# VectorE exp tiles planned eight units ahead in a fused attention and gated-MLP block

## The chip, the cores and the metric

The kernel runs on one core of a Trainium2 chip. The metric is the time of one execution on the device in microseconds (us). Before the change it is 927.56 us, the median of 4 runs (927.19 to 927.69).

## The reference

One transformer block on a sequence of 2048 tokens of width 640, one batch, bf16 inputs. Layer norm, attention with 32 heads of size 20, residual, layer norm, gated MLP of width 1728, residual:

```python
x = A_x                                               # [1, 2048, 640]
qkv = layernorm(x) @ wqkv                             # 32 heads, Dh = 20
p = softmax(q k^T * Dh ** -0.5)                       # per head 2048 x 2048
h = x + (p v, heads joined) @ wo
n = layernorm(h)
out = h + (gelu_tanh(n @ w_gate) * (n @ w_up)) @ w_down
```

## The kernel before

**Tiling.** The queries are cut into seven chunks of 512, 512, 256, 256, 256, 128 and 128 rows (`CHUNKS`). Heads go in groups of four, since four heads of 20 rows fit in the 128 rows of TensorE's array. A *slot* is one chunk with one head group (512 rows), two groups (256) or four (128); so every slot has 64 score tiles of 128 x 512, and there are 32 slots (8, 8, 4, 4, 4, 2, 2 by chunk). In the code and in the diff "group" in "end of a group" is such a slot.

**Units.** The tiles that ScalarE exponentiates are taken in *units* of alternately three and two tiles, 719 units in all, numbered here from 0. `unit(u)` (line 833) queues one: the score matmuls (L852, into PSUM banks 0 to 2 or 3 and 4), one ScalarE exp over the whole unit (L339, PSUM to the buffers `pts` or `rege`), and then the PV matmuls (L339 too, `ps<-pts,v_all` or `ps<-rege,v_all`), which add up P times V in PSUM bank 6. The exp buffers hold 18 tiles, about seven units: an exp must wait for the PV that reads the tiles it overwrites. The scores of unit u reuse the banks of unit u-2, so they wait until exp u-2 is done.

**VectorE exp tiles.** Eight of a slot's 64 tiles (two in the first slot) are exponentiated by VectorE instead: 250 tiles. Their scores go to a free bank (7 or 5), VectorE reads them (L812, one 128 x 512 instruction a tile), and for each pair of tiles it runs seven instructions of 1024 columns (bit arithmetic on int16, L339) in `d_exp`. The pair buffers hold four pairs. `dtile[u]` names the VectorE tile that goes with unit u; `D_FIRST` and `D_SPAN` spread a slot's tiles over its units. A finished tile joins the PV of a unit that is at least `D_LAG` = 8 units later; at the last PV of a slot all that are left are flushed.

**Slot end.** `epilogue` copies bank 6 out (`osb`), transposes it (L962), and multiplies by the reciprocal of the row sums (L968, L971) into `o_nat`. After a chunk's last slot, `post` does that chunk's output projection (L616, `wo`), residual, LN2, gate matmuls (L1039), gelu (ScalarE, with table loads for gelu and back to exp), up matmuls (L1039, multiplied by VectorE at L1085), down matmuls (L1096) and output. That work is spread among the exps of the following chunks; that of the last chunk (`tail`) runs after the last exp, with gelu straight from PSUM (L1061, L1064).

**What sets the order.** Every operation is put into `Sched` with its engine, an estimated duration, a priority and its dependences. `schedule()` walks time with those estimates, lets each engine take the ready operation of best priority (scores 0, PV 1, epilogue and VectorE tiles 2, output projection and LN2 2.5, background 3), and so fixes one instruction order per engine; `emit` writes it with semaphore waits. Nothing is reordered on the chip: an instruction that waits holds what is queued behind it on its engine.

**Zero matmuls.** Two rules in `schedule()` add matmuls that change nothing. When a PV operation is placed and PE's planned use over the last 3.4 us is under `PAD_MIN`, groups of four matmuls with a zero stationary operand into bank 6 are put behind it (`ps<-kt_all,zer`, L339). When PE has nothing ready and the use is under `WARM_MIN`, one such group, or one 128 x 512 matmul into bank 7 (`ps<-kt_all`), is put in.

The two lines that the change turns most on:

```python
want = min(nd, (k[0] - D_FIRST) * nd // D_SPAN + 1) if k[0] >= D_FIRST else 0   # VectorE tiles due by unit k[0] of a slot
if len(quads) < PV_QUADS and not final:      # PV_QUADS = 2: a PV waits until it has two quads of tiles
```

Of the kernel before, what the change touches and what calls it, by code (L numbers as in the profile page):

```python
# [14 lines left out]
SEM_LAT = {("act", "pe"): 0.056, ("dve", "pe"): 0.058, ("pe", "act"): 0.045, ("pe", "dve"): 0.038}  # L15
SEM_ANY = 0.036
DRAIN = {"pe": 0.165, "act": 0.115, "dve": 0.085, "pool": 0.05, "sp": 0.0}
WARM_WIN, WARM_MIN = 3.4, 0.5
PAD_WIN, PAD_MIN = 3.4, 0.42
PE_AGE = 1.5  # L20

MODE_SWITCH = {"pe": 0.105, "act": 1.28}
# [19 lines left out]
class Sched:  # L42
# [12 lines left out]
    def op(self, eng, fns, dur, prio, reads=(), writes=(), acq=(), rel=(), after=(), sem=None, lat=None, mode=None, util=0.0):  # L55
        o = Op()
        o.i = len(self.ops)
        o.eng, o.dur, o.lat, o.sem = eng, dur, DRAIN[eng] if lat is None else lat, sem
        o.util = util
        o.mode = mode  # L60
        o.tag = writes[0] if writes else None
        o.fns = fns if isinstance(fns, list) else [fns]
        o.prio = (prio, o.i)
        deps = set(after)
        for r in reads:
            if r in self.lw:
                deps.add(self.lw[r])
        for w in writes:
            if w in self.lw:
                deps.add(self.lw[w])  # L70
            deps.update(self.rd.get(w, ()))
        for r in reads:
            self.rd.setdefault(r, []).append(o.i)
        for w in writes:
            self.lw[w] = o.i
            self.rd[w] = []
        deps.discard(o.i)
        o.deps = deps
        o.acq = list(acq)
        o.rel = list(rel)  # L80
        o.succ = []
        o.ready = 0.0
        self.ops.append(o)
        return o.i

    def schedule(self):
# [22 lines left out]
        while done < total:  # L109
# [4 lines left out]
            for e in ENGINES:  # L114
                while future[e] and future[e][0][0] <= t + 1e-9:
                    _, p, i = heapq.heappop(future[e])
# [6 lines left out]
                while ready[e]:  # L123
                    p, i = heapq.heappop(ready[e])
                    o = ops[i]
# [35 lines left out]
                if chosen is None:  # L161
                    if e == "pe" and self.warm is not None:
# [5 lines left out]
                        if sum(x for _, x in recent) < WARM_MIN * WARM_WIN and (free7 or live):  # L168
                            o = Op()
# [14 lines left out]
                o = chosen  # L184
                if e == "pe" and self.pad is not None and o.tag and o.tag[0] == "O":
                    while recent and recent[0][0] < t - PAD_WIN:
                        recent.popleft()
                    u = sum(x for _, x in recent) + o.util
                    while u < PAD_MIN * PAD_WIN and o.util < 1.1:
                        o.fns = o.fns + self.pad  # L190
                        o.dur += 0.215
                        o.util += 0.213
                        u += 0.213
                    live = o.i not in self.final
# [100 lines left out]
CHUNKS = tuple((sum(SIZES[:i]), n) for i, n in enumerate(SIZES))  # L295
# [10 lines left out]
PV_QUADS = 2  # L306
D_LAG = 8
# [1 line left out]
ND = 4  # L309
D_PER_SLOT = (8,) * len(SIZES)  # L310
D_SLOT0 = 2
D_FIRST, D_SPAN = 1, 16
RSQRT_MAGIC = float(0x5F3759DF)

P_QK, P_PV, P_PRO, P_EPI, P_LN, P_BG = 0, 1, 1.5, 2, 2.5, 3
# [2 lines left out]
def bass_sequential_preLN__mha_block__glu_gated_geglu__prompt_kernel(  # L318
# [12 lines left out]
    with ExitStack() as es:  # L331
# [6 lines left out]
        def I(method, *args, **kwargs):  # L338
            return lambda eng: getattr(eng, method)(*args, **kwargs)  # L339
# [414 lines left out]
        slots = []  # L754
        for c, (q0, nq) in enumerate(CHUNKS):
            n = 512 // nq
            slots += [(c, tuple(range(g, g + n))) for g in range(0, NG, n)]

        tiles = []
# [4 lines left out]
            slot_end.append(len(tiles))  # L764

        PAT = [((0, 1, 2), (3, 4))] * len(CHUNKS)
        units, ubank, dtile, ends = [], [], [], []
        i, in_slot = 0, {}
        while i < len(tiles):
            s_ = tiles[i][0]  # L770
            c = slots[s_][0]
            bs = PAT[c][len(units) % 2]
            k = in_slot.setdefault(s_, [0, 0])
            nd = D_PER_SLOT[c] if s_ else D_SLOT0
            units.append(tiles[i:i + len(bs)])
            ubank.append(bs[0])
            i += len(units[-1])
            want = min(nd, (k[0] - D_FIRST) * nd // D_SPAN + 1) if k[0] >= D_FIRST else 0
            if k[1] < want and tiles[i][0] == s_:
                dtile.append(tiles[i])  # L780
                k[1] += 1
                i += 1
            else:
                dtile.append(None)
            k[0] += 1
            ends.append(i)
        assert all(k[1] % 2 == 0 for k in in_slot.values())
        d_tiles = set(x for x in dtile if x)
        x_unit = {}
        for u, tl in enumerate(units):  # L790
# [2 lines left out]
        pv_bank = {}  # L793
# [3 lines left out]
        d_raw, d_done = [], []  # L797
# [33 lines left out]
        def unit(u):  # L831
            tl = units[u]
# [8 lines left out]
            pb, o = (pts, p0) if p0 < PR else (pts2, p0 - PR)  # L841
# [35 lines left out]
            n = 512 * na  # L877
# [6 lines left out]
            while pv_wait:  # L884

                quads = []
                while pv_wait and len(quads) < PV_QUADS:
                    x0 = pv_wait[0][2]
                    have = [x for x in pv_wait if x[2][:3] == x0[:3]]
                    want = 4 - sum(1 for j in range(4) if x0[:3] + (j,) in d_tiles)  # L890
                    if len(have) < want or quads and quads[0][0][2][0] != x0[0]:
                        break
                    del pv_wait[0:want]
                    quads.append(have)
                if not quads:
                    return
                s_ = quads[0][0][2][0]
                c, gs = slots[s_]
                q0, nq = CHUNKS[c]
                nk = 512 // nq  # L900
                final = quads[-1][0][2][1:3] == (gs[-1], NT // nk - 1)
                if len(quads) < PV_QUADS and not final:
                    pv_wait[0:0] = [x for h in quads for x in h]
                    return

                for have in quads:
                    for x in list(d_done):
                        if u - x_unit[x[2]] >= D_LAG and x[2][3] not in [y[2][3] for y in have]:
                            have.append(x)
                            d_done.remove(x)  # L910
                while final and d_done:
                    have = []
                    for x in list(d_done):
                        if x[2][3] not in [y[2][3] for y in have]:
                            have.append(x)
                            d_done.remove(x)
                    quads.append(have)
                if s_ not in pv_bank:
                    pv_bank[s_] = bk = Bank(6)
                    acq = [bk]  # L920
                else:
                    bk, acq = pv_bank[s_], []
                fns, reads = [], ["vones", "zer"] + k_keys[0][0]
                for have in quads:
                    for kk in range(nk):
                        for pt, pkey, (_, g, kb, j) in have:
                            kt = kb * nk + kk
                            o = 512 * 6 + nq * gs.index(g)
                            fns.append(I("matmul", PS[32 * j:32 * j + VW, o:o + nq], v_all[:, kt, 4 * g + j, :],
                                         pt[:, kk * nq:(kk + 1) * nq], start=(s_, j) not in pv_open, stop=(kt == NT - 1),  # L930
                                         tile_position=(0, 32 * j), skip_group_check=True))
                            pv_open.add((s_, j))
                            reads += [pkey, ("v", kt, g // 4)]
                pv = op("pe", fns, 0.218 * len(quads), P_PV, mode="col", util=0.213 * len(quads), reads=reads, writes=[("O", s_), "pvseq"], acq=acq)
                if final:
                    sc.final.add(pv)
                    assert not d_done and not d_raw
                    epilogue(s_, bk)


        def base(c):
            n = CHUNKS[c][1]
            if n == 128:
                return 2 + (c == len(CHUNKS) - 1)
            return 2 * (c % 2) if n < 512 else 0

        def epilogue(s_, bk):
            s = s_ % 2
# [29 lines left out]
        def prefetch(c):  # L978
            q0, nq = CHUNKS[c]
            nt = nq // 128  # L980
            tb = base(c)
            op("sp", I("dma_start", h_sb[:, tb:tb + nt, :], x_hbm[q0:q0 + nq, :].rearrange("(t p) d -> p t d", p=128)), 0.08, P_EPI,
               writes=[("h", tb + tt, hf) for tt in range(nt) for hf in range(2)], sem=f"xr{c}", lat=2.0 + nq * 0.0034,
               after=tuple(e_ops) + tuple(w_readers) if c == 0 else ())

        def post(c, banks, tail):
            p = P_EPI if tail else P_LN
            q0, nq = CHUNKS[c]
            nt = nq // 128
            tb = base(c)  # L990
            hb = 1792 * tb
            first = tuple(e_ops) + tuple(last_qk[0]) + tuple(d_ops) if c == 0 else ()
# [129 lines left out]
        for s_, (c, gs) in enumerate(slots):  # L1122
# [27 lines left out]
            while ui < len(units) and ends[ui] - len(units[ui]) < slot_end[s_]:  # L1150
                unit(ui)
                ui += 1
# [35 lines left out]
```

## Time and profile before

| | |
|---|---|
| median of 4 runs | 927.56 us (927.19 to 927.69) |
| profiled execution | 927.6 us, of which the span from first to last instruction is 925.6 us |
| ScalarE (ACT) | 885.7 us busy, 96% |
| TensorE (PE) | 845.5 us busy, 91%; granted clock 1.000 |
| VectorE (DVE) | 810.4 us busy, 88% |
| DMA | 34.36 MB, 37 GB/s on the mean |
| first exp starts, last exp ends | 35.93 us, 889.49 us |
| exps of 1536 and of 1024 columns | 1590 and 1170 ns each, overlapping: 2.26 us for one of each on the chain |

The page gives busy times over the whole span. The views by stage split it at the first and the last exp. "L339" is the line of the helper that records most operations, so its groups are told apart by engine and by the names behind it (output`<-`inputs). PEld is TensorE's weight load, which runs beside the matmuls. A line's "idle before" is the time in which its engine had nothing running, and the name behind `<-` is what ended it.

### The profile page before, as it was taken

The numbers are of one execution on the slowest core, as the hardware profiler recorded it, in microseconds if no ns is written. First come the engines' busy times: TensorE is split into PE (matmuls) and PEld (weight loads), VectorE is DVE, ScalarE is ACT, GpSimd is POOL, SyncE is SP. The second block draws the span as 40 slices with busy tenths as digits, with TensorE's granted clock in tenths as the row PEclk, the third lists the DMA queues.
The fourth block names the chain that finished last, engine by engine and source line by source line (L and its number), as shares of the span: only waits on it lengthen the run. The fifth ranks groups of instructions, "written<-read, shape, count | busy, mean of one in ns | idle before, by whom it ended". The sixth has DMA issues, their size and how long they took to land.

```text
span 925.6 us, 23154 instructions
## 1 busy us (share of the span) xinstructions
PE 845.5 (91%) x10109; PEld 354.9 (38%) x10109; DVE 810.4 (88%) x1703; ACT 885.7 (96%) x801; POOL 35.1 (4%) x117
## 2 busy tenths in 40 slices
PE   3998999999998998999888999999989999999998
PEld 2432222222232222233233333344444445555667
DVE  7859999999898998888798997989998997998873
ACT  6899999999999999999999999999999999999962
POOL 5000000000001000000001000001000000000100
DMA  7211010322550000001011000000100000110000
GB/s 256 87 26 44 18 55 18 90 60 66 147 185 16 15 1 1 1 15 44 1 31 23 9 2 1 16 30 10 37 16 16 8 23 2 31 32 10 10 17 16
DMA packets 39517, 34.36 MB, mean 37 GB/s; under 512 B 19436, under 2 KB 36936, under 8 KB 39416
## 3 DMA queue, kind: packets, MB, share of 16 engines
q1 hardware_dynamic: 39416, 32.89, 12.6%
q8 instruction: 79, 1.29, 0.6%
q14 instruction: 22, 0.18, 0.1%
HBM read 20.12 MB, written 8.09 MB: 30 GB/s over the span
## 4 chain that ended last, share of the span: by engine, by line
ACT 72%; PE 14%; DVE 11%; issue 1%; POOL 0%; DMA 0%
ACT pts L339 46%; ACT rege L339 25%; PE ps L1039 4%; DVE qt_all L339 3%; PE ps L616 3%; PE ps L852 3%; PE ps L339 3%; DVE rege L339 2%; PE ps L1096 2%; DVE qt_all L812 1%; DVE rege L812 1%; DVE stats L339 1%; ACT L339 1%; DVE rege L1074 1%; PE ps L561 0%
## 5 line engine op out<-in xcount | busy, mean ns | idle before, releaser
L339 ACT ACTIVATE pts<-ps 128x1536 bf16<-128x1536 f32 x480 | 573.1, 1380 | 4.9 <-PE ps L852 3.7
L852 PE MATMUL ps<-qt_all,kt_all 32*128 32x256 bf16 (+2 forms) x3584 | 303.4, 289 | 43.1 <-ACT pts L339 27.4
L339 ACT ACTIVATE rege<-ps 128x1536 bf16<-128x1536 f32 x239 | 300.1, 1381 | 1.9 <-PE ps L339 1.5
L852 PEld LDWEIGHTS ps<-qt_all,kt_all 32*128 32x128 bf16 x3584 | 95.1, 92 | 276.8 <-ACT pts L339 161.1
L339 DVE TENSOR_TENSOR qt_all<-qt_all 128x1024 bf16<-128x1024 bf16 (+1 forms) x240 | 164.1, 684 | 3.4
L1039 PE MATMUL ps<-rege,regw 128*128 128x256 bf16 (+2 forms) x980 | 154.6, 290 | 9.9 <-ACT rege L339 4.1
L339 PE MATMUL ps<-pts,v_all 128*21 128x256 bf16 (+2 forms) x2098 | 138.8, 290 | 0.5 <-DVE rege L339 0.5
L812 DVE TENSOR_SCALAR rege<-ps 128x512 int16<-128x512 f32 x154 | 105.4, 685 | 27.6 <-PE ps L852 26.9
L339 DVE TENSOR_SCALAR qt_all<-qt_all 128x1024 bf16<-128x1024 int16 (+1 forms) x288 | 115.8, 417 | 2.5
L339 PE MATMUL ps<-rege,v_all 128*21 128x256 bf16 (+2 forms) x1294 | 113.3, 292 | 0.1
L1039 PEld LDWEIGHTS ps<-rege,regw 128*128 128x128 bf16 x980 | 72.5, 98 | 67.9 <-issue 28.5
L616 PE MATMUL ps<-regw 128*128 128x512 bf16 (+1 forms) x360 | 87.1, 352 | 2.0 <-DVE v_all L749 0.7
L1096 PE MATMUL ps<-regw,rege 128*128 128x320 bf16 x448 | 79.4, 301 | 1.1 <-DVE rege L1064 0.5
L812 DVE TENSOR_SCALAR qt_all<-ps 128x512 int16<-128x512 f32 x96 | 65.7, 685 | 3.7 <-PE ps L852 2.6
L339 DVE TENSOR_SCALAR rege<-rege 128x1024 int16<-128x1024 int16 (+2 forms) x166 | 67.2, 421 | 1.3
L339 DVE TENSOR_TENSOR rege<-rege 128x1024 bf16<-128x1024 bf16 (+3 forms) x103 | 65.5, 644 | 0.9
L339 PEld LDWEIGHTS ps<-pts,v_all 128*21 128x21 bf16 x2098 | 50.2, 91 | 37.2 <-issue 31.6
L339 PE MATMUL ps<-kt_all,zer 128*32 128x512 bf16 x676 | 56.6, 384 | 0.0
L1096 PEld LDWEIGHTS ps<-regw,rege 128*128 128x128 bf16 x448 | 36.7, 97 | 32.4 <-issue 15.8
L339 PEld LDWEIGHTS ps<-rege,v_all 128*21 128x21 bf16 x1294 | 41.0, 91 | 20.6 <-issue 14.3
L1085 DVE TENSOR_TENSOR rege<-rege,ps 128x512 bf16<-128x512 bf16 (+1 forms) x53 | 35.8, 676 | 12.1 <-PE ps L1039 11.8
L616 PEld LDWEIGHTS ps<-regw 128*128 128x128 bf16 x360 | 28.6, 99 | 45.4 <-issue 21.3
(95 smaller groups left out, 574.5 us busy)
## 6 DMA issues: line engine op xcount, KB each, us to landing
rege<-in_A_x_dram SPq DMA_DIRECT2D x6, 640.0 KB, 5.1
q_rows<-regw SPq DMA_DIRECT2D x20, 128.0 KB, 1.7
out_dram<-rege SPq DMA_DIRECT2D x16, 160.0 KB, 2.0
regw<-in_B_w_gate_dram SPq DMA_DIRECT2D x1, 2160.0 KB, 12.0
regw<-in_B_w_up_dram SPq DMA_DIRECT2D x1, 2160.0 KB, 17.0
regw<-in_B_w_down_dram SPq DMA_DIRECT2D x1, 2080.0 KB, 22.2
kt_all<-k_rows SPq DMA_DIRECT2D x12, 160.0 KB
qt_all<-q_rows SPq DMA_DIRECT2D x12, 160.0 KB
```

The source lines that it names most:

```text
L339: return lambda eng: getattr(eng, method)(*args, **kwargs)
L616: yield op("pe", lambda eng, l=l, r=r, k=k: eng.matmul(bank(bk, n), l, r, start=(k == 0), stop=(k == len(steps) - 1)), c_mm(n), prio, mode ...
L812: d_ops.append(op("dve", lambda eng: eng.tensor_scalar(v[:, 512 * h:512 * h + 512], bank(b), EXP_MUL, -32000.0, ALU.mult, ALU.max), c_dve( ...
L852: return lambda eng: eng.matmul(out()[:, kk * nq:(kk + 1) * nq], kt_all[32 * j:32 * j + 32, g, kt * 128:(kt + 1) * 128], qt_all[32 * j:32 ...
L1039: op("pe", lambda eng, a=a, f=f, fi=fi: eng.matmul(bank(bk)[:, fi * nq:(fi + 1) * nq], w[:, a, F0[f]:F0[f] + 128], hnT[:, a, 128 * tb:128 ...
L1074: cp.append(op("dve", lambda eng, bg=bg, fv=fv, w=w: eng.tensor_copy(fv, bank(bg, w)), c_dve(w), p, reads=[kg], writes=hkeys(k), rel=[bg], ...
L1085: hdone.append(op("dve", lambda eng, bu=bu, fv=fv, w=w: eng.tensor_tensor(fv, fv, bank(bu, w), ALU.mult), c_dve(w), p, reads=[ku] + hkeys( ...
L1096: op("pe", lambda eng, f=f, o=o, hf=hf, bk=bk: eng.matmul(bank(bk, 320), ha_f[:, o:o + 128], wd[:, f, hf * 320:(hf + 1) * 320], start=(f = ...
```

## The change

Four things change; none of the arithmetic does.

- The VectorE tiles of a slot are planned over 20 units instead of 16 (`D_SPAN`), and then each is taken eight units sooner (`D_LEAD`), so that a slot's first ones go with units of the slot before it. Chunk 1's don't go ahead of chunk 1's first unit. A finished tile that has waited 12 units or more (`D_LAG` + `D_HOLD`) gets a PV quad of its own, and tiles are only given to the PV of their own slot.
- A slot's first PV may have one quad instead of two.
- The thresholds of the zero matmuls rise: 0.42 to 0.5 behind a PV, to 0.6 behind a slot's last PV, and 0.5 to 0.55 where PE has nothing ready.
- `base()`, which places a chunk in the buffers of the MLP, is written in another way.

```diff
--- before.py
+++ after.py
@@ -15,8 +15,8 @@
 SEM_LAT = {("act", "pe"): 0.056, ("dve", "pe"): 0.058, ("pe", "act"): 0.045, ("pe", "dve"): 0.038}
 SEM_ANY = 0.036
 DRAIN = {"pe": 0.165, "act": 0.115, "dve": 0.085, "pool": 0.05, "sp": 0.0}
-WARM_WIN, WARM_MIN = 3.4, 0.5
-PAD_WIN, PAD_MIN = 3.4, 0.42
+WARM_WIN, WARM_MIN = 3.4, 0.55
+PAD_WIN, PAD_MIN, PAD_END = 3.4, 0.5, 0.6
 PE_AGE = 1.5
 
 MODE_SWITCH = {"pe": 0.105, "act": 1.28}
@@ -186,7 +186,8 @@
                     while recent and recent[0][0] < t - PAD_WIN:
                         recent.popleft()
                     u = sum(x for _, x in recent) + o.util
-                    while u < PAD_MIN * PAD_WIN and o.util < 1.1:
+                    want = PAD_END if o.i in self.final else PAD_MIN
+                    while u < want * PAD_WIN and o.util < 1.1:
                         o.fns = o.fns + self.pad
                         o.dur += 0.215
                         o.util += 0.213
@@ -309,7 +310,7 @@
 ND = 4
 D_PER_SLOT = (8,) * len(SIZES)
 D_SLOT0 = 2
-D_FIRST, D_SPAN = 1, 16
+D_FIRST, D_SPAN, D_LEAD, D_HOLD = 1, 20, 8, 4
 RSQRT_MAGIC = float(0x5F3759DF)
 
 P_QK, P_PV, P_PRO, P_EPI, P_LN, P_BG = 0, 1, 1.5, 2, 2.5, 3
@@ -764,7 +765,7 @@
             slot_end.append(len(tiles))
 
         PAT = [((0, 1, 2), (3, 4))] * len(CHUNKS)
-        units, ubank, dtile, ends = [], [], [], []
+        units, ubank, dplan, ends = [], [], [], []
         i, in_slot = 0, {}
         while i < len(tiles):
             s_ = tiles[i][0]
@@ -776,15 +777,20 @@
             ubank.append(bs[0])
             i += len(units[-1])
             want = min(nd, (k[0] - D_FIRST) * nd // D_SPAN + 1) if k[0] >= D_FIRST else 0
-            if k[1] < want and tiles[i][0] == s_:
-                dtile.append(tiles[i])
+            if k[1] < want and i < len(tiles) and tiles[i][0] == s_:
+                dplan.append((len(units) - 1, tiles[i]))
                 k[1] += 1
                 i += 1
-            else:
-                dtile.append(None)
             k[0] += 1
             ends.append(i)
         assert all(k[1] % 2 == 0 for k in in_slot.values())
+        chunk_u = [min(u for u, tl in enumerate(units) if slots[tl[0][0]][0] == c) for c in range(len(CHUNKS))]
+        dtile = [None] * len(units)
+        u = 0
+        for n, x in dplan:
+            u = max(n - D_LEAD, u, D_FIRST, chunk_u[1] if slots[x[0]][0] == 1 else 0)
+            dtile[u] = x
+            u += 1
         d_tiles = set(x for x in dtile if x)
         x_unit = {}
         for u, tl in enumerate(units):
@@ -899,19 +905,26 @@
                 q0, nq = CHUNKS[c]
                 nk = 512 // nq
                 final = quads[-1][0][2][1:3] == (gs[-1], NT // nk - 1)
-                if len(quads) < PV_QUADS and not final:
+                if len(quads) < PV_QUADS and not final and s_ in pv_bank:
                     pv_wait[0:0] = [x for h in quads for x in h]
                     return
 
                 for have in quads:
                     for x in list(d_done):
-                        if u - x_unit[x[2]] >= D_LAG and x[2][3] not in [y[2][3] for y in have]:
+                        if u - x_unit[x[2]] >= D_LAG and x[2][0] == s_ and x[2][3] not in [y[2][3] for y in have]:
                             have.append(x)
                             d_done.remove(x)
-                while final and d_done:
+                if any(x[2][0] == s_ and u - x_unit[x[2]] >= D_LAG + D_HOLD for x in d_done):
                     have = []
                     for x in list(d_done):
-                        if x[2][3] not in [y[2][3] for y in have]:
+                        if x[2][0] == s_ and u - x_unit[x[2]] >= D_LAG and x[2][3] not in [y[2][3] for y in have]:
+                            have.append(x)
+                            d_done.remove(x)
+                    quads.append(have)
+                while final and any(x[2][0] == s_ for x in d_done):
+                    have = []
+                    for x in list(d_done):
+                        if x[2][0] == s_ and x[2][3] not in [y[2][3] for y in have]:
                             have.append(x)
                             d_done.remove(x)
                     quads.append(have)
@@ -934,15 +947,16 @@
                 pv = op("pe", fns, 0.218 * len(quads), P_PV, mode="col", util=0.213 * len(quads), reads=reads, writes=[("O", s_), "pvseq"], acq=acq)
                 if final:
                     sc.final.add(pv)
-                    assert not d_done and not d_raw
+                    assert not any(x[0] == s_ for x in d_raw)
                     epilogue(s_, bk)
 
 
         def base(c):
             n = CHUNKS[c][1]
-            if n == 128:
-                return 2 + (c == len(CHUNKS) - 1)
-            return 2 * (c % 2) if n < 512 else 0
+            if n == 512:
+                return 0
+            half = sum(1 for _, m in CHUNKS[:c] if m == 256) % 2
+            return 2 * half + (n == 128 and CHUNKS[c - 1][1] == 128)
 
         def epilogue(s_, bk):
             s = s_ % 2
```

## The prediction

> **What bounds the kernel now.** I read the page first (share of each engine, chain that ended last), then busy time by stage, then ScalarE's own waits, then the timeline around the longest of them and around the end.
>
> ```profile
> PE 845.5 (91%) x10109; PEld 354.9 (38%) x10109; DVE 810.4 (88%) x1703; ACT 885.7 (96%) x801; POOL 35.1 (4%) x117
> ACT 72%; PE 14%; DVE 11%; issue 1%; POOL 0%; DMA 0%
> ```
>
> ScalarE carries the chain: 72% of the span.
>
> ```profile
> 35.90:250.00 214.10, 200.40 (x1593) 60.01 (x1592) 191.40 (x400) 211.61 (x187) 0.62 (x1) 1.00 0.20 54
> 250.00:889.50 639.50, 593.02 (x7940) 256.97 (x7938) 574.49 (x1174) 638.52 (x557) 22.39 (x84) 1.00 0.09 24
> 889.50:925.60 36.10, 30.73 (x428) 25.56 (x426) 14.33 (x35) 11.02 (x14) 0.00 (x0) 1.00 0.04 15
> ```
>
> The columns are stretch, length, then busy us (count) of PE, PEld, DVE, ACT, POOL, then the granted TensorE clock. Between 35.9 and 889.5 us, the exp stage, ScalarE is busy 850.1 of 853.6 us. In the last 36.1 us it is busy 11.0, and PE 30.7.
>
> ```profile
> ACT rege L339 <- PE ps L339: 1.5, 1, 1.5
> ACT pts L339 <- PE ps L339: 0.9, 2, 0.6
> ACT rege L339 <- PE ps L852: 0.4, 1, 0.4
> ```
>
> These are ScalarE's waits inside that stage (the one 3.7 us wait for L852 there is the first exp). A wait for "PE ps L339" is a wait for the PV matmuls that read an exp buffer which the next exp overwrites. The longest:
>
> ```profile
> 143.03 0.39 PE L852 MATMUL ps<-qt_all,kt_all 32*128 32x512 bf16 x2
> 143.36 0.60 PE L339 MATMUL ps<-pts,v_all 128*21 128x512 bf16 x5
> 144.44 2.37 ACT L339 ACTIVATE rege<-ps 128x1536 bf16<-128x1536 f32 x2 [1.46 <-PE ps L339]
> ```
>
> Exp 94 waits for 11 PV matmuls that stand in PE's queue behind the scores of unit 95, and those scores could only start when exp 93 was done: score wait, scores, 0.99 us of PV, 1.46 us idle. Last, the end, as the chain and then as ScalarE's timeline:
>
> ```profile
> 887.73 3.37 PE ps L1096 x24
> 891.32 1.00 PE ps L339 x48
> 902.51 2.79 PE ps L1039 x50
> 907.48 3.80 PE ps L1096 x28
> 911.28 7.05 PE ps L1039 x126
> 918.83 3.99 PE ps L1096 x28
> ```
>
> ```profile
> 895.72 0.70 ACT L567 ACTIVATE rege<-ps 128x640 bf16<-128x640 bf16 x1 [4.71 <-PE ps L561]
> 896.44 1.28 ACT L339 ACT_TABLE_LOAD   x1
> 900.59 1.70 ACT L339 ACTIVATE rege<-rege 128x1792 bf16<-128x1792 bf16 x1 [2.87 <-DVE rege L1074]
> 902.30 1.28 ACT L339 ACT_TABLE_LOAD   x1
> 903.59 0.20 ACT L339 ACTIVATE sd<-sd 128x1 bf16<-128x1 bf16 x1
> 905.62 0.70 ACT L567 ACTIVATE rege<-ps 128x640 bf16<-128x640 bf16 x1 [0.30 <-PE ps L561]
> ```
>
> The last exp ends at 889.49. Chunk 5's MLP then still owes 70 gate matmuls, its gelu and everything after; the last chunk's own MLP (the 126) starts only at 911.28.
>
> **The sum to work against.** 35.9 head + 853.6 exp stage + 36.1 tail = 925.6 span, 2.0 around it, 927.6 for the profiled run; the median is 927.56, so the two can be used alike.
>
> **The change, part by part.** I compared the instruction order of both programs as built. DVE has 1705 instructions in both, POOL 121, SP 180; 719 exps and 250 VectorE exp tiles in both. So ScalarE's exp work changes by 0. What differs: 272 more zero matmuls (68 groups of four), 18 more warm matmuls, one table load less (15 for 16), and the order.
>
> *Zero and warm matmuls.* 676 now are busy 56.6 us, 0.335 a group; 55 warm ones 16.7 us, 0.304 each. Added: 68 x 0.335 + 18 x 0.304 = 28.3 us of PE. The cover is PE's idle time before scores that wait for ScalarE, 161.1 + 77.2 us (PEld waits, L852): 238 us. Cost 0 while covered, up to 28.3 without. Few stretches get long: one gap between scores holds eight groups, others at most five. The gain is 0 too: the granted clock is 1.00 in every stretch, and no matmul group after 20 us runs at half rate. The Trainium skill ("TensorE: Matmul & The Clock Gate", "Part 1: The HAM clock gate") has PE fall to half clock after an idle window of some 3.4 us; by it the additions would insure matmuls, but this trace shows nothing to insure.
>
> *VectorE exp tiles eight units ahead, spread over 20 units instead of 16.* Two effects.
>
> (a) Inside the exp stage. PE runs in order, so I looked for exps whose buffer is freed by a PV standing behind the scores of their own or the next unit. Before: exps 50, 94, 139, 274, 475; their idle: 0.57 + 1.46 + 0.38 + about 0 + 0.13 = 2.5 us. After: exps 22, 26 and 203 behind the *next* unit's scores; 30, 57, 85, 113, 533 behind their own. In the first group's units 18 to 30 the extra VectorE chain comes between the casts of V, so PV comes at units 18, 23, 27 where it came at 16, 20, 23, 26. Prices from the 1.46 row: with 8 PV (0.55 on the chain) instead of 11 (0.99), 1.46 - 0.44 = 1.0 each for exps 22 and 26; 1.5 for 203 (15 PV, waiting for VectorE); 0.6 for 30 and 0.4 for 85, like the 0.57 and 0.38 rows; 57, 113 and 533 have a long exp ahead of them that covers scores and 8 PV, so 0 unless VectorE is late: 0.2 each. Sum 5.1, net **+2.6**. Below: -1 if the planner's order leaves ScalarE ahead; above: all eight at 1.46 = 11.7, net +9.2.
>
> The other losses of the stage: 359.5 exp pairs at 2.26 (the chain's piece) are 812.5, tables and gelus between chunks 36.1, so 853.6 holds 5.0 of loss, 2.5 beyond the five waits. Of these, two finals that wait for a VectorE chain (exps 206 and 430, 0.08 and 0.37 idle, 0.35 and 0.64 late) have their tiles done earlier: **-1.0**. But 73 PVs wait on VectorE where 43 did; the PE rows show such waits cost little now (0.5 and 1.0 us in all), so 0 for them, +4 at worst; -2.5 at best.
>
> One VectorE read of scores (unit 197) must wait for a PV of unit 199, since all eight held tiles are taken; behind it VectorE's queue stands for two units. It is inside the 1.5 of exp 203. K and Q of a group are now needed earlier (units 24 to 19, 69 to 63, 92 to 89, 136 to 130) by a VectorE tile's scores on PE. The tightest: the third K step's last transfer is issued at 135.0, lands about 137 (1.7 us on the page's row for such stores), and unit 89 is at about 137. Price 0, at worst 2.
>
> (b) At the end. Chunk gelus come earlier (after 678 exps instead of 692 in chunk 4), and chunk 5's gate matmuls almost end with the scores: after the last scores PE has 19 gates, no L1096, then PV; before, 24 L1096 and all 70 gates. Walk, on the old clock with the last exp ending at 889.5. PV: 32 of 48 are already past, the rest ends at 889.95 (before 892.3). Output copy 0.69, transposes 0.6, reciprocal 0.25, four multiplies 0.68: 892.4 (before 894.9). ScalarE meanwhile does table load, gelu 1.70, table load, 0.2: free at 894.0; it evacuates at 894.0 (before 895.72). wo, adds, statistics with one up-multiply between them: sqrt at 899.75 (before 903.59, which stood behind gelu and two table changes). Apply and transposes: 901.4; evacuation 901.5 (before 905.62). PE still owes 23 L1096 (3.2): 904.6; then all 140 of the last MLP at 0.056 = 7.8: 912.4 (before 918.33). **-5.9**. Floor: the 24 L1096 and 51 gates leave the tail in any case, but partly ran under the last exps: -3.4, the chain's 3.37. Ceiling -7.5, if the waits between also close.
>
> The missing table load is in this walk at 1.28, its row. By the Trainium skill ("ScalarE: Activation LUTs", "What ACT_TABLE_LOAD costs") a set switch costs about 2.66 with its drain; taken so, the end would be 1.4 better still; but here the load starts 0.02 after the last exp, so I take the row.
>
> *First PV of a group by one quad* is inside (a): 8 PV can become 4, 0.3 less. The new form of base() gives the same offsets for these seven chunks: 0.
>
> **Sum:** 927.6 + 2.6 - 1.0 - 5.9 = **923.3**.
>
> **Rivals.** (1) The waits in (a) do not come, since the early PVs are ready when VectorE is less crowded: 927.6 - 1 - 2.5 - 5.9 = 918, lower still with the ceiling. For: VectorE idles 26.9 us in the stage waiting for scores. Against: the order fixes 22, 26 and 203. (2) No change that can be measured (0.2%, 925.7 to 929.4, is what a measurement here can tell): the tail gives only 3.4 and (a) takes 2.6 to 4: about 927. (3) Slower: PE, in order, stands at PVs that wait for VectorE. Place: units 18 to 30 and the first group heads up to unit 204. Price: 11.7 - 2.5 = +9.2, less 5.9 and 1.0 = 929.9; with the +4 of the later waits 933.9. It decides from 7.7 us of added exp-stage loss on. For: 73 against 43 such waits, and two long new runs behind the next scores at the very start. Against: after exp 204 only one such place (533) is left.
>
> **Numbers.** My forecast 0.57 (919 to 925.7), rival 1 0.10, rival 2 0.14, rival 3 0.19: faster 0.67, same 0.14, slower 0.19. Range 917.5 to 930.5: to rival 1's value below and just past rival 3's 929.9 above.
>
> **What would show it.** Tail from last exp to end 30 instead of 36.1 us; first chunk's stage (exps 0 to 187) 2 to 4 us longer, with ScalarE waits for PE ps L340 near exps 22, 26 and 203; granted clock still 1.00; gelu of 1792 right after the last exp. Wrong if the tail shrinks by under 3, or if the exp stage changes by more than 6.

## The result, and the profile after

The changed kernel takes 929.06 us, the median of 34 runs (926.51 to 931.85), beside 927.51 us for the kernel before (55 runs, 926.52 to 930.04). The ratio is 1.0013, 95% interval 1.0007 to 1.0018: slower, by 1.5 us between the medians, where 923.3 was forecast. The profiled execution took 927.95 us with a span of 926.1. The median lies above the profiled execution because the TensorE clock was halved for one short stretch in over half of the changed kernel's executions: of the 35 whose clock is on record, 20 with a mean granted clock of 0.998 (one of them 0.996) have a median of 929.39 us, 15 with 1.000 one of 927.81. The kernel before, in 39 executions at 1.000 beside the experiments, has 927.43. So at the full clock the two are only 0.4 us apart, less than either one's runs scatter; most of the 1.5 us is in the half-clock stretches, and what the prediction missed is the gain that did not come.

The page's first lines and its chain that ended last, of after:

```profile
PE 878.4 (95%) x10399; PEld 371.1 (40%) x10399; DVE 815.9 (88%) x1703; ACT 888.3 (96%) x800; POOL 37.5 (4%) x117
ACT 59%; PE 29%; DVE 10%; DMA 2%; issue 0%; SPq 0%
ACT pts L340 38%; ACT rege L340 20%; PE ps L858 9%; PE ps L1110 6%; PE ps L1053 5%; PE ps L340 5%; PE ps L617 3%; DVE qt_all L340 3%; DVE rege L340 3%; DMA regw<-in_A_wqkv_dram 1%; DVE rege L818 1%; ACT L340 1%; DVE qt_all L818 1%; PE ps L562 0%; PE ps L976 0%
```

ScalarE's share of the chain fell from 72% to 59% and TensorE's rose from 14% to 29%. The score matmuls, now L858, hold 9% of it; as L852 they held 3%. TensorE is busy 32.9 us more, and zero matmuls are only part of that. The costliest groups of the page, first before, then after:

```profile
L852 PE MATMUL ps<-qt_all,kt_all 32*128 32x256 bf16 (+2 forms) x3584 | 303.4, 289 | 43.1 <-ACT pts L339 27.4
```

```profile
L858 PE MATMUL ps<-qt_all,kt_all 32*128 32x256 bf16 (+2 forms) x3584 | 334.3, 288 | 18.5 <-ACT pts L340 8.3
L340 PE MATMUL ps<-kt_all,zer 128*32 128x512 bf16 x948 | 77.9, 384 | 0.0
```

The same 3584 score matmuls, each as long as before (288 against 289 ns), cover 30.9 us more. "Busy" counts time in which at least one runs, so fewer of them now run side by side. The zero matmuls add 77.9 - 56.6 = 21.3 us.

By stage (length, then busy us and count of PE, PEld, DVE, ACT, POOL, then the granted clock), of after:

```profile
36.30:250.00 213.70, 207.56 (x1678) 62.61 (x1674) 191.28 (x399) 210.59 (x185) 0.62 (x1) 1.00 0.20 57
250.00:896.50 646.50, 626.08 (x8263) 276.71 (x8267) 583.16 (x1181) 643.52 (x559) 24.74 (x84) 1.00 0.09 24
896.50:926.10 29.60, 23.14 (x326) 19.40 (x314) 11.29 (x29) 9.56 (x14) 0.00 (x0) 0.99 0.04 12
```

The tail fell from 36.1 to 29.5 us. The exp stage grew from 853.6 to 860.2: it took back all that the tail gave. ScalarE's waits in that stage, of after (total us, times, longest):

```profile
ACT rege L340 <- PE ps L340: 2.5, 2, 1.4
ACT pts L340 <- PE ps L340: 1.8, 3, 1.0
ACT rege L340 <- PE ps L858: 0.2, 1, 0.2
```

The waits for L340, the PV matmuls, explain 1.7 us of the 6.6 (4.2 of idle behind PV against 2.5). Idle time ended by score matmuls and others adds 0.7 (1.26 against 0.55, with the first exp left out). The rest, some 4 us, is in no idle time. ScalarE's exps overlap: one that follows an idle time lasts 1.451 us, and the next can start 1.331 us after it, so a delay of up to 0.12 us leaves no idle at all. It shows in the length of the records. The exps into `pts` by shape (up to 889 us), before and then after:

```profile
L339 ACT ACTIVATE pts<-ps 128x1536 bf16<-128x1536 f32 x240 | 381.6, 1590 | 4.4 <-PE ps L852 3.7 <-PE ps L339 0.6
L339 ACT ACTIVATE pts<-ps 128x1024 bf16<-128x1024 f32 x240 | 280.8, 1170 | 0.5 <-PE ps L339 0.4
```

```profile
L340 ACT ACTIVATE pts<-ps 128x1536 bf16<-128x1536 f32 x238 | 359.9, 1512 | 6.3 <-PE ps L858 4.0 <-PE ps L340 1.5
L340 ACT ACTIVATE pts<-ps 128x1024 bf16<-128x1024 f32 x238 | 259.4, 1090 | 0.3 <-PE ps L340 0.3
```

A record that lasts 1.59 us instead of 1.451 began while the exp ahead of it was still running: its scores were there in time. After, the mean falls to 1512 and 1090 ns. The exps are not faster, they start later. To put a number on it I took the interval from one exp's start to the next and subtracted the shortest spacing (1.331 us after 1536 columns, 0.904 after 1024). The excesses under 0.4 us are called *small waits* below. They sum to 8.2 us before and 13.3 after, and 9.6 of the 13.3 belong to exps that start before the one ahead has ended. Excesses of 0.4 us and over, most of them late PVs, sum to 4.1 and 6.0. So small waits grew by 5.1 us and the longer ones by 1.9; together that is 0.4 more than the 6.6 of the stage. The time around gelus and table loads is in neither sum. The sums of small waits hold to about 0.7 us: with these two spacings and every pair of neighbouring exps counted they are 8.6 before and 13.5 after.

### The profile page after: what moved, and what is told of

The parts are those of the page before. It is cut to its first block, busy times and chain, and to the rows that moved or that the text cites. A ratio compares the mean times of both kernels' runs of the same rounds, so it can differ in the third digit from the quotient of the medians.

```text
span 926.1 us, 23729 instructions
## 1 busy us (share of the span) xinstructions
PE 878.4 (95%) x10399; PEld 371.1 (40%) x10399; DVE 815.9 (88%) x1703; ACT 888.3 (96%) x800; POOL 37.5 (4%) x117
## 4 chain that ended last, share of the span: by engine, by line
ACT 59%; PE 29%; DVE 10%; DMA 2%; issue 0%; SPq 0%
ACT pts L340 38%; ACT rege L340 20%; PE ps L858 9%; PE ps L1110 6%; PE ps L1053 5%; PE ps L340 5%; PE ps L617 3%; DVE qt_all L340 3%; DVE rege L340 3%; DMA regw<-in_A_wqkv_dram 1%; DVE rege L818 1%; ACT L340 1%; DVE qt_all L818 1%; PE ps L562 0%; PE ps L976 0%
## 5 line engine op out<-in xcount | busy, mean ns | idle before, releaser
L340 ACT ACTIVATE pts<-ps 128x1536 bf16<-128x1536 f32 x480 | 564.7, 1301 | 6.6 <-PE ps L858 4.0
L858 PE MATMUL ps<-qt_all,kt_all 32*128 32x256 bf16 (+2 forms) x3584 | 334.3, 288 | 18.5 <-ACT pts L340 8.3
L340 ACT ACTIVATE rege<-ps 128x1536 bf16<-128x1536 f32 x239 | 290.3, 1299 | 2.9 <-PE ps L340 2.5
L858 PEld LDWEIGHTS ps<-qt_all,kt_all 32*128 32x128 bf16 x3584 | 110.9, 92 | 244.7 <-ACT pts L340 119.1
L340 DVE TENSOR_TENSOR qt_all<-qt_all 128x1024 bf16<-128x1024 bf16 (+1 forms) x240 | 164.5, 685 | 4.5
L340 PE MATMUL ps<-pts,v_all 128*21 128x256 bf16 (+2 forms) x2098 | 140.9, 290 | 0.0
L818 DVE TENSOR_SCALAR rege<-ps 128x512 int16<-128x512 f32 x154 | 105.5, 686 | 32.2 <-PE ps L858 30.9
L340 DVE TENSOR_SCALAR qt_all<-qt_all 128x1024 bf16<-128x1024 int16 (+1 forms) x288 | 118.7, 417 | 3.4
L340 PE MATMUL ps<-rege,v_all 128*21 128x256 bf16 (+2 forms) x1294 | 114.2, 292 | 0.4 <-DVE osb L340 0.4
L1053 PEld LDWEIGHTS ps<-rege,regw 128*128 128x128 bf16 x980 | 73.1, 98 | 65.7 <-issue 29.5
L340 PE MATMUL ps<-kt_all,zer 128*32 128x512 bf16 x948 | 77.9, 384 | 0.0
L340 DVE TENSOR_SCALAR rege<-rege 128x1024 int16<-128x1024 int16 (+2 forms) x166 | 67.8, 421 | 1.3
L340 PEld LDWEIGHTS ps<-pts,v_all 128*21 128x21 bf16 x2098 | 50.2, 91 | 44.6 <-issue 33.7
L340 DVE TENSOR_TENSOR rege<-rege 128x1024 bf16<-128x1024 bf16 (+3 forms) x103 | 66.0, 645 | 1.2
L1110 PEld LDWEIGHTS ps<-regw,rege 128*128 128x128 bf16 x448 | 36.7, 98 | 34.1 <-issue 19.0
L340 PEld LDWEIGHTS ps<-rege,v_all 128*21 128x21 bf16 x1294 | 39.1, 91 | 23.5 <-issue 16.9
```

The source lines that it names most:

```text
L818: d_ops.append(op("dve", lambda eng: eng.tensor_scalar(v[:, 512 * h:512 * h + 512], bank(b), EXP_MUL, -32000.0, ALU.mult, ALU.max), c_dve( ...
L858: return lambda eng: eng.matmul(out()[:, kk * nq:(kk + 1) * nq], kt_all[32 * j:32 * j + 32, g, kt * 128:(kt + 1) * 128], qt_all[32 * j:32 ...
L1053: op("pe", lambda eng, a=a, f=f, fi=fi: eng.matmul(bank(bk)[:, fi * nq:(fi + 1) * nq], w[:, a, F0[f]:F0[f] + 128], hnT[:, a, 128 * tb:128 ...
L1110: op("pe", lambda eng, f=f, o=o, hf=hf, bk=bk: eng.matmul(bank(bk, 320), ha_f[:, o:o + 128], wd[:, f, hf * 320:(hf + 1) * 320], start=(f = ...
```

## The experiments

All numbers of the table come from each kernel's runs and its profiled execution; "score busy" is the busy time of the score matmuls, "PV idle" ScalarE's idle time ended by PV matmuls. The kernel before, run beside them, had medians of 927.43 to 927.65. The profiled executions of before_same_rows, after_free_row, pick_head_48 and span21_two_quads have one to three stretches at half clock, that of zeros_unsent many; the others have none between 21 us and their last microsecond.

| kernel | median us | ratio (95%) | stage | tail | small waits | PV idle | score busy | zero busy |
|---|---|---|---|---|---|---|---|---|
| before | 927.51 | | 853.6 | 36.1 | 8.2 | 2.5 | 303.4 | 56.6 |
| after | 929.06 | 1.0013 (1.0007 to 1.0018) | 860.2 | 29.5 | 13.3 | 4.2 | 334.3 | 77.9 |
| after_other_rows | 923.06 | 0.9951 (0.9940 to 0.9963) | 854.9 | 29.5 | 7.5 | 4.2 | 306.0 | 78.0 |
| before_same_rows | 932.98 | 1.0070 (1.0052 to 1.0088) | 859.3 | 36.3 | 13.3 | 2.7 | 340.4 | 57.2 |
| after_old_zeros | 930.86 | 1.0038 (1.0026 to 1.0050) | 861.2 | 30.0 | 13.6 | 5.2 | 336.3 | 59.1 |
| before_new_zeros | 931.66 | 1.0050 (1.0037 to 1.0062) | 860.1 | 34.0 | 8.1 | 6.2 | 307.3 | 73.9 |
| zeros_unsent | 970.52 | 1.0480 (1.0448 to 1.0512) | 899.8 | 29.5 | 16.6 | 7.8 | 358.0 | 0 |
| lead_0 | 943.18 | 1.0170 (1.0156 to 1.0184) | 872.9 | 32.2 | 7.2 | 20.1 | 301.7 | 70.9 |
| after_free_row | 944.16 | 1.0182 (1.0168 to 1.0195) | 870.6 | 36.3 | 9.4 | 9.6 | 308.5 | 90.5 |
| pick_head_48 | 925.63 | 0.9977 (0.9968 to 0.9986) | 857.9 | 30.6 | 8.3 | 6.2 | 305.6 | 76.0 |
| pick_head_span21 | 925.42 | 0.9972 (0.9962 to 0.9982) | 856.2 | 30.4 | 7.6 | 4.4 | 302.6 | 83.4 |
| span21_two_quads | 930.39 | 1.0028 (1.0017 to 1.0039) | 862.4 | 31.6 | 7.7 | 7.9 | 308.2 | 75.3 |

**What the score matmuls do.** A score matmul uses 32 of the array's rows, those of its head's number in the group (0 to 3), and tiles follow one another through the four numbers. PE's timeline (start and length in us, engine, line, operation, count) shows what follows from that. Score matmuls of a unit alone (x3), or of three tiles of a unit and one for VectorE (x4), before and then after:

```profile
300.57 0.40 PE L852 MATMUL ps<-qt_all,kt_all 32*128 32x512 bf16 x4
302.83 0.40 PE L852 MATMUL ps<-qt_all,kt_all 32*128 32x512 bf16 x4
```

```profile
299.67 0.61 PE L858 MATMUL ps<-qt_all,kt_all 32*128 32x512 bf16 x4 [0.42 <-ACT rege L340]
301.93 0.61 PE L858 MATMUL ps<-qt_all,kt_all 32*128 32x512 bf16 x4
304.19 0.39 PE L858 MATMUL ps<-qt_all,kt_all 32*128 32x512 bf16 x3
```

Before, the VectorE tile is the one that comes next after its unit's tiles, so its head number is a free one, and four matmuls take 0.40 us, as three do. After, the tile stands eight units earlier, behind a unit whose tiles are unrelated to it. In 204 of 250 cases (7 before) it has, in PE's order, the head number of a tile of the unit it stands behind; the fourth matmul then starts 0.22 us later, on rows that are in use, and the four take 0.61. The Trainium skill ("TensorEngine Tiling (Array Packing)", "Key Properties") says that different tiles of the array can run matmuls in parallel; the rows here agree, and add the price where the tile is the same one. That a VectorE tile of 512 columns costs PE 0.2 us instead of nothing was not in the forecast. Two kernels test it alone, each in the unchanged instruction order.

*after_other_rows:* after, with the scores of each VectorE tile computed from the Q and K rows of a head that its unit doesn't use.

```diff
-            def qk_mms(out, x, kk):
+            def qk_mms(out, x, kk, row=None):
...
+                j = j if row is None else row
...
+                row = min(j for j in range(4) if j not in [x[3] for x in tl])
-                qd = op("pe", [qk_mms(lambda: bank(bd), xd, kk) for kk in ...
+                qd = op("pe", [qk_mms(lambda: bank(bd), xd, kk, row) for kk in ...
```

> The changed kernel, with the order on every engine kept, but the scores of each VectorE tile are taken from a head whose 32 rows of the array the unit's own score matmuls leave free (so they are another head's scores: the output is not the reference's). In the changed kernel 204 of the 250 VectorE tiles share their 32 rows with a score matmul of the unit they stand behind, in the kernel before 7; here 29. Theory A (shared rows put the score matmuls one after another, and the 0.1 to 0.2 us that PE loses per tile comes back as many small ScalarE waits): busy time of the score matmuls falls from 334 to about 305 us, the exp stage from 860.2 to about 857, total 3 us lower, about 926. Rival B (the zero matmuls cost it): no change, 929. Rival C (late PVs alone): no change, 929.

Measured: 923.06 us; in its profile score busy falls to 306.0 and small waits to 7.5, with the late PVs as they were (4.2). The chain is ScalarE's again:

```profile
ACT 85%; PE 9%; DVE 6%; issue 0%
L859 PE MATMUL ps<-qt_all,kt_all 32*128 32x256 bf16 (+2 forms) x3584 | 306.0, 289 | 34.5 <-ACT pts L340 18.1
```

*before_same_rows:* before, with those scores computed from the rows of the unit's first head (`row = tl[0][3]`, the rest as above).

> The kernel before, with its order on every engine kept, but the scores of each VectorE tile are taken from the head of the unit's first tile, so that 248 of 250 share rows with the unit's own score matmuls (another head's scores: the output is not the reference's). Theory A: busy time of the score matmuls rises from 303 to about 335 us, the exp stage by 3 us, total about 930.5. Rivals B and C: no change, 927.5.

Measured: 932.98 us, 5.5 more than before; score busy 340.4, small waits 13.3. Its chain has moved as after's did:

```profile
ACT 45%; PE 32%; DVE 20%; issue 1%; POOL 1%; DMA 1%; DVEq 0%
L853 PE MATMUL ps<-qt_all,kt_all 32*128 32x256 bf16 (+2 forms) x3584 | 340.4, 288 | 22.9 <-ACT pts L339 14.4
```

So sharing rows costs 5.5 to 6.0 us, seen from either side, with no change in the order of any engine. That is twice the 3 us that was expected of each. Without it the change is worth 4.4 us.

**The zero matmuls.** *after_old_zeros:* the thresholds of before in after, which leads to another planned order too.

```diff
-WARM_WIN, WARM_MIN = 3.4, 0.55
-PAD_WIN, PAD_MIN, PAD_END = 3.4, 0.5, 0.6
+WARM_WIN, WARM_MIN = 3.4, 0.5
+PAD_WIN, PAD_MIN, PAD_END = 3.4, 0.42, 0.42
```

> The changed kernel with the thresholds of the zero and warm matmuls as before (0.42, 0.5, none at a slot's end): 744 zero matmuls instead of 948 and 54 warm ones instead of 73. Rival B (zero matmuls delay scores): 2 to 4 us lower, 925 to 927. Theory A and rival C: within 1 us of 929.

Measured: 930.86 us, 1.8 more than after and 0.9 over what Theory A and rival C allowed. Zero matmuls are busy 18.8 us less and small waits don't fall (13.6 against 13.3): the added ones hold up no scores that matter. Four of its five runs have a clock under 1.000, three of them 0.996; the one at 1.000 took 928.49.

*before_new_zeros:* the new thresholds alone in before.

```diff
-WARM_WIN, WARM_MIN = 3.4, 0.5
-PAD_WIN, PAD_MIN = 3.4, 0.42
+WARM_WIN, WARM_MIN = 3.4, 0.55
+PAD_WIN, PAD_MIN, PAD_END = 3.4, 0.5, 0.6
...
+                    want = PAD_END if o.i in self.final else PAD_MIN
-                    while u < PAD_MIN * PAD_WIN and o.util < 1.1:
+                    while u < want * PAD_WIN and o.util < 1.1:
```

> The kernel before with the changed kernel's thresholds for zero and warm matmuls alone: 876 zero matmuls instead of 676. By order the late PVs are at exps 50, 117, 139, 162 (own scores), 206 and 654 (next unit's). PE's work after the last scores 28.7 us instead of 30.7. Zero matmuls without a cost: tail -2, late PVs +1 to +2, total 926 to 928.5. Zero matmuls that delay scores: 930 or more. Fewer runs with a granted clock under 1.000 than the 1 in 5 of the kernel before.

Measured: 931.66 us, in the range that was given to zero matmuls that delay scores, but not for that reason: small waits are 8.1 (8.2 before), so the zeros themselves are again hidden. The planner's order, which the zeros' estimated time shifts, is worse. One of its five runs has a clock under 1.000, where fewer than 1 in 5 were expected. PV idle is 6.2 instead of 2.5, and one unit's scores stand behind 15 output-projection matmuls that were placed ahead of them. PE's timeline and then ScalarE's, of before_new_zeros:

```profile
139.99 2.59 PE L617 MATMUL ps<-regw 128*128 128x320 bf16 x15
142.51 0.60 PE L853 MATMUL ps<-qt_all,kt_all 32*128 32x512 bf16 x6
```

```profile
142.95 2.36 ACT L340 ACTIVATE pts<-ps 128x1536 bf16<-128x1536 f32 x2 [2.55 <-PE ps L853]
```

*zeros_unsent:* after, in its order, but with no zero or column warm matmul sent.

```diff
-                        o.fns = o.fns + self.pad
...
-                order.append(o)
+                if not (o.tag == "warm" and o.mode == "col"):
+                    order.append(o)
```

> The changed kernel with every zero matmul (the 948 into bank 6) planned but not sent: the order of all else is the same on each engine. If zero matmuls delay scores (rival B), the small waits of ScalarE (13.3 us in the changed kernel) fall to 9 or less and the total to 924 to 926. If they only hold the clock, the small waits stay at 12 to 13.5, the granted clock has windows at half speed inside the exp stage in most runs (about 1.5 us each, the difference between the changed kernel's runs at 1.000 and at 0.998), and the total is 931 to 940.

Measured: 970.52 us, 41.5 over after, and 30 over the top of what was expected. Small waits rise to 16.6 instead of falling; the lower clock adds to them, so this run alone does not settle whether zero matmuls hold up scores. The mean granted clock is 0.919 (0.902 to 0.919 in six runs). The worst stretch, in zeros_unsent and then the same in after:

```profile
476.00:483.00 7.00, 6.35 (x38) 1.38 (x37) 3.81 (x7) 6.84 (x7) 0.00 (x0) 0.50 0.01 2
483.00:513.00 30.00, 27.79 (x283) 10.76 (x284) 23.92 (x51) 26.16 (x24) 0.00 (x0) 0.69 0.14 23
```

```profile
476.00:483.00 7.00, 6.63 (x98) 2.99 (x94) 6.97 (x18) 7.00 (x7) 0.00 (x0) 1.00 0.01 4
483.00:513.00 30.00, 28.53 (x419) 11.76 (x419) 27.99 (x62) 30.00 (x28) 4.51 (x14) 1.00 0.12 24
```

From 467.5 us on the clock is at half for 34.1 us on end, and ScalarE loses 3.84 of the 30 us after 483.

**The lead.** *lead_0:* after, with each VectorE tile taken with its own unit.

```diff
-D_FIRST, D_SPAN, D_LEAD, D_HOLD = 1, 20, 8, 4
+D_FIRST, D_SPAN, D_LEAD, D_HOLD = 1, 20, 0, 4
```

> The changed kernel with D_LEAD = 0: VectorE tiles over 20 units, none ahead. 9 tiles share rows. PE's work after the last scores 25.8 us. By order 12 exps wait for a PV behind the next unit's scores and some 8 behind their own, where the changed kernel has 3 and 5. If such places cost 1.0 to 1.5 and 0.3 us each, ScalarE idles 14 to 18 us for PV, and the total is 931 to 937. If the eight units ahead are what shortens the tail, the tail is 36 us; by the work left it should be 32.

Measured: 943.18 us, 6 over the expected top. Only 9 tiles share rows, score busy is 301.7, and ScalarE waits for PV 19 times in the exp stage, 20.1 us where 14 to 18 were expected:

```profile
ACT pts L340 <- PE ps L340: 13.4, 14, 2.2
ACT rege L340 <- PE ps L340: 6.7, 5, 2.0
```

With the tiles spread over 20 units and no lead, PVs hold up exps. The lead removes 16 us of such idle time (20.1 to 4.2). The tail is 32.2, as expected from PE's work left: of its 6.6 us gain, 3.9 come without the lead.

**Repairs.** *after_free_row:* a VectorE tile is delayed to the first unit that does not use its rows.

```diff
+            while any(y[3] == x[3] for y in units[u]):
+                u += 1
             dtile[u] = x
```

> The changed kernel, but each VectorE tile goes with the first unit, from the planned one on, that has no tile of the same head number j; the output is the reference's. 20 tiles share rows instead of 204. The order moves with it: by order seven exps wait for a PV behind the next unit's scores (22, 26, 90, 99, 208, 211, 651), where three did. Theory A: score matmuls busy about 305 us, 3 us from the small waits, but 2 to 4 back through the late PVs: 926 to 930. Rival B: 929 or more. The small waits (under 0.4 us each) should fall by a third or more under theory A alone.

Measured: 944.16 us, where an improvement was expected. The rows did come free (20 tiles share, score busy 308.5, small waits 9.4), but the exps then stand elsewhere: excesses of 0.4 us and over sum to 20.2 us, with 9.6 us idle behind PV and 7.8 of other idle; the tail is back at 36.3, and the mean clock is 0.993 (three stretches at half clock). That the delay of tiles makes those PVs late is the likely reading; it was not taken apart further.

*pick_head_48* and *pick_head_span21:* the VectorE tile of a unit is picked, among the unit's tiles and the next one, so that its head number is free in the unit eight places earlier. The first also has `PAD_MIN` 0.48, the second `D_SPAN` 21.

```diff
-                dplan.append((len(units) - 1, tiles[i]))
+                at = max(len(units) - 1 - D_LEAD, 0)
+                pool = units[-1] + [tiles[i]]
+                x = next((y for y in reversed(pool) if y[3] not in [z[3] for z in units[at]]), tiles[i])
+                units[-1] = [y for y in pool if y != x]
+                dplan.append((len(units) - 1, x))
```

> A repair with the reference's output: the changed kernel, but of the tiles that stand next in order, the one whose head number the unit eight units earlier does not have becomes the VectorE tile (35 of 250 share rows instead of 204); the zero matmuls' threshold behind a PV is 0.48, with which PE's work after the last scores is the same 23.1 us as in the changed kernel. Late PVs by order: exps 22, 26, 80, 214 behind the next unit's scores, 30, 113, 200 behind their own. Theory A (shared rows cost 6 us): score matmuls busy 305 to 310 us, tail 30 us, total 922 to 925. If shared rows don't matter outside the run with another head's rows: 929.

> The same repair with the old thresholds of the change and the VectorE tiles spread over 21 units instead of 20: 23 tiles share rows; late PVs by order at only 30 and 203 (behind the next unit's scores) and 113; PE's work after the last scores 24.7 us. Theory A with the late PVs priced as before (1.0 and 1.4 us, 0.3): ScalarE's idle for PV about 2.7 us instead of 4.3, tail 31 us, total 921 to 924. Rival: as the row above.

Measured: 925.63 and 925.42 us, each just above its expected range, with 35 and 23 tiles that share rows and small waits of 8.3 and 7.6. What keeps back the rest was not tried alone; PV idle (6.2 and 4.4, where 2.7 was expected of the second) and the runs with a short stretch at half clock (6 of 11 and 5 of 8) are what the record shows. The three runs of pick_head_span21 at clock 1.000 have a median of 923.73. It computes the whole reference, and it beats before (0.9972, 0.9962 to 0.9982) and so after.

*span21_two_quads:* pick_head_span21, with a slot's first PV waiting for two quads as in before.

```diff
-                if len(quads) < PV_QUADS and not final and s_ in pv_bank:
+                if len(quads) < PV_QUADS and not final:
```

> The repaired kernel with 21 units (925.4) with the first PV of a slot waiting for two quads again. 31 tiles share rows, PE's work after the last scores 25.8 us (24.7), late PVs by order at 24, 27, 204 behind the next unit's scores and 75, 81, 215 behind their own (30, 203 and 113). If the one-quad rule matters: 927 to 929, of it 1 in the tail and 1.5 to 2 in waits for PV. If not: 925 to 926.

Measured: 930.39 us, 5.0 over pick_head_span21. One wait for PV of 4.1 us has come in:

```profile
ACT pts L340 <- PE ps L340: 7.9, 3, 4.1
```

## Why the prediction was wrong, step by step

**The step that failed** is part (a) of the VectorE tiles, in a term that the sum put at nothing without a reason. It followed what a tile's exp, its PV and its buffers wait for, and priced nothing for where its own score matmuls run. There the price is 5.8 us: small waits 13.3 with the shared rows, 7.5 without (5.3 if every pair of neighbouring exps is counted). The stage was forecast at 853.6 + 2.6 - 1.0 = 855.2; after_other_rows has 854.9, after 860.2. Total: 923.3 forecast, 923.06 with the rows free; two of those five runs, with no stretch at half clock, are at 921.5 and 921.7, so the other terms were some 1.7 too high in sum, and that the medians match so closely is luck. That leaves no room for a large cost of the parts priced at 0, `base()` and the earlier need of K and Q; neither was tried alone. The pair of exps at 2.26 us, from which the forecast worked out a loss of 5.0 us in the stage, hid this kind of delay: the shortest pair is 1.331 + 0.904 = 2.235, and the difference over 359.5 pairs, 9.0 us, is about the small waits that before already had (8.2). The missing term had a row in the trace of before: four score matmuls in 0.40 us are only possible if they run side by side, and the change broke up the tiles that did.

**Late PVs: right, 0.9 too high.** ScalarE's timeline of after shows the idle times where the order put them, exps 22, 26, 30 and 203:

```profile
62.46 2.36 ACT L340 ACTIVATE rege<-ps 128x1536 bf16<-128x1536 f32 x2 [1.04 <-PE ps L340]
68.12 2.36 ACT L340 ACTIVATE pts<-ps 128x1536 bf16<-128x1536 f32 x2 [1.04 <-PE ps L340]
73.17 2.37 ACT L340 ACTIVATE pts<-ps 128x1536 bf16<-128x1536 f32 x2 [0.42 <-PE ps L340]
272.39 1.02 ACT L340 ACTIVATE rege<-ps 128x1024 bf16<-128x1024 f32 x1 [1.43 <-PE ps L340]
```

They were priced at 1.0, 1.0, 0.6 and 1.5; exp 85 at 0.4 (0.32 measured), and 57, 113 and 533 at 0.2 each (none). Sum 4.2 for 5.1. The first chunk's stage (exps 0 to 187) grew by 1.6 us, from 215.5 to 217.1, where 2 to 4 were forecast, and the whole stage by 6.6, over the 6 that the forecast had named as a sign of being wrong.

**The tail: right.** 29.5 us for 30, a gain of 6.6 for 5.9. The gelu of 1792 columns runs straight after the last exp, with one table load of 1.28 us ahead of it and no other wait:

```profile
896.56 1.28 ACT L340 ACT_TABLE_LOAD   x1
897.86 1.70 ACT L340 ACTIVATE rege<-rege 128x1792 bf16<-128x1792 bf16 x1
899.57 1.28 ACT L340 ACT_TABLE_LOAD   x1
900.98 0.69 ACT L568 ACTIVATE rege<-ps 128x640 bf16<-128x640 bf16 x1
```

The tail goes with PE's work that is left: PE is busy 23.1 us after the last exp here and 30.7 before, and the tail is that time plus 4.7 to 6.6 us in every kernel of the table.

**The zero matmuls: cost right, the reason for no gain wrong.** Their added 21.3 us were hidden, as the forecast had it. "This trace shows nothing to insure" took the clock of 1.00 as given without them, but in after the zero matmuls hold it: with all 948 left out, zeros_unsent takes 41.5 us more. Before was not tried without its 676. Whether the *higher* thresholds buy anything stays open. after_old_zeros has only one run of five at a full clock, of 928.49 us against after's 927.81, and its order differs too; that it has more runs under 1.000 (4 of 5 against 20 of 35) would speak for a gain, on few runs. The half-clock stretches of zeros_unsent come in multiples of 3.413 us, but in its exp stage PE never idled for more than 2.4 us at once and was busy 92% of the time. The page "TensorE: Matmul & The Clock Gate" of the Trainium skill (Part 1: The HAM clock gate) puts the fall to half clock after an idle window of about 3.4 us. Here the clock fell without 3.4 us of idling.

**First PV by one quad: too small.** It was put at 0.3 us within (a). In the repaired kernel it is worth 5.0, the other order that the planner makes around it included.

**The two finals' VectorE waits, -1.0.** No longer in ScalarE's waits, as forecast; not tried alone.

**The rivals.** Rival 3 had the sign, and its cause is refuted: PV idle rose by 1.7 us, where its case needed 7.7. Rival 2 had about the value, for another reason: it let the tail give only 3.4, and the tail gave 6.6.

**What stays open:** why after has a half-clock stretch in more of its runs, and where it falls. Of the kernel before, 2 of the 41 runs beside the experiments have one, of after 20 of 35, of lead_0 none of four. Of the 55 runs of before beside the result, whose clocks are not on record, 11 lie at 928.97 us or more and the others at 928.05 or less, so its share may be larger than 2 of 41. Among the profiled executions, pick_head_48 has one stretch of 3.4 us in the tail, where PE pauses for the last output copy (clock 0.77 from 896 to 900 us); before_same_rows and span21_two_quads have one of 3.4 us inside the exp stage, and after_free_row has three there. By the medians at the two clocks it costs after 1.6 us, enough for the 1.1 us between its profiled execution, 927.95, and its median.

## What to carry to other kernels

When an operation is moved to another neighbour, look at what it shared with the old one: matmuls on 32 rows run side by side only if they use different rows, and a busy time that is less than count times duration is the sign in the profile. A producer with 95% of its time taken delays its consumer in steps of 0.1 us that no idle time shows; compare start-to-start spacings, or the mean length of overlapping records. And before calling filler work useless because the clock is full, take it out once.

## What the runs showed of the hardware

- Score matmuls on different 32-row strips start 0 to 20 ns apart and run together; on the same strip, 512 columns wide, 220 to 239 ns apart. In after 74 consecutive pairs are that far apart and 2 more 200 to 219 ns, in before 1 and 6.
- At half clock TensorE still shows 91% busy (6.35 of 7.00 us at clock 0.50) since each matmul's record is longer (583 ns on the mean in that window, 291 in after), so busy time says little of the load. Counting matmuls does: 38 in that window against 98 in after, 12 of them zero matmuls.
- One stretch of 3.4 us at half clock costs about 1.5 us of the total, in a kernel that ScalarE mostly bounds (after, 929.29 at 0.998 against 927.81 at 1.000; 2.0 in pick_head_span21, by the medians at the two clocks).
